# Stages B to F of a transformer block's backward pass on one core: new homes for transposed tiles, smaller loads, another queue for late transposes and stores

## The chip, the core and the metric

The kernel runs on one core of one Trainium2 chip. The metric is device time in microseconds (us), median over several executions. The page of a profile gives the "span" from the first to the last instruction; the time is some 1.7 us more. Each execution also records the mean granted clock of the matmul engine (TensorE).

## The reference

Forward and backward of one block: layer norm, linear attention with 32 heads of 20, output projection, residual, layer norm, gated MLP, residual. Outputs are the result and the gradients of x, wqkv, wo, w1, w3 and w2.

```python
x = A_x                                                # [1, 2048, 640] bf16
h = x + _A_ref(_layernorm(x), A_wqkv, A_wo)            # pq, pk = phi(q), phi(k); o = (pq.kv) / (pq.z)
h2 = h + _B_ref(_layernorm(h), A_w1, A_w3, A_w2)       # (silu(h.w1) * (h.w3)).w2, F = 1728   [names shortened]
_out, _vjp = jax.vjp(_f, A_x, A_wqkv, A_wo, B_w1, B_w3, B_w2)
return (_out, *_vjp(grad_out))
```

## The kernel before

The kernel fixes the order of instructions itself. The core's engines are TensorE (the matmul engine), VectorE, ScalarE, GpSimd and SyncE. SyncE issues almost all DMAs (transfers between the chip's main memory and the core's own; some transpose on the way), in the order of the text. A DMA that waited held up those behind it in that queue: in stage D below, one load is issued at 618.6 us behind two others that waited until 611.4 us. A tile framework adds the waits. Names: hh is the MLP's product and hb its transpose; g2 the output gradient; ggb the gradients at w1 and w3; g_h the gradient of h and ghT its transpose; gnd the gradient of the attention's numerator and denominator, gndT its transpose; pqb and pkb are rows of pq and pk. After stage A (forward and first half of the MLP's backward, to 361 us) come:

**Stage B**, the gradient of w2, and in its shadow the loads for C:

```python
load_hh(0)                                   # hb: 512 columns of hh, transposed by DMA
# [cut]
load_hh(1); load_hh(2)
for fc in range(FT):                         # 14 chunks of 128 rows, the last has FL = 64
    acc = ps.tile([P, 2, 512], F32, name="gw", bufs=4)
    for j in range(2):
        for t in range(ST):
            T.matmul(acc[:n, j, 0:HD], lhsT=hb[b][:, t, i*P:i*P+n], rhs=g2[:, t, j*HD:(j+1)*HD], ...)
    # [cut: copy to gw2o, store from ScalarE]
    if fc < CT: kvbd_T(*BLOCKS[fc])          # transposes of kv on the matmul engine
    if fc == 3: load_hh(3)
    if fc == 5: load_w13()                   # w13a, w13b: transposed by DMA
    if fc == 8: load_gg(0)                   # 1728 KB each
    if fc == 11: load_gg(1)
    if fc == FT - 2: w13_tail()
```

**Stage C**, one tile of 128 rows per step:

```python
for t in range(ST):
    b_load(t + 2); b_load_q(t - 1)                           # hnb, o_sb, pqb
    if t % 2 == 0 and 2 <= t <= ST - 4: load_gg(t // 2 + 1)  # for tiles t+2, t+3
    # three of six parts of ghn(t): 54 matmuls of 320 columns
    ln_rest.pop(t - 1)(); b_gT(t - 1)        # ghT: DMA transpose on SyncE
    b_gkv(t - 3)                             # part of ghn(t)
    b_go(t - 2)                              # reads ghT(t-2); part of ghn(t)
    b_gpq(t - 3)                             # reads gndT(t-3); part of ghn(t)
    b_gndT(t - 2)                            # gndT: DMA transpose on SyncE
```

**Stage D**, gradients of k and v; kT of chunk 3 takes the slot that chunk 0 leaves:

```python
    gphi(vaT[c][...], gkvT, pkb[c][:, i, :], g_k[:, t, :], d_acc)
    if t == TPC - 1: load_kT(3, ba, "ggb", 2)    # two DMA transposes
    if i == 3 and c + 2 < SC: load_pk(c + 2)     # pkb for tiles 8 to 11, then 12 to 15
```

**Stage E** is the gradient of x, with the last jobs of dwqkv between; **stage F** is 60 jobs of 16 matmuls for dw1 and dw3, on blocks of 288 columns loaded through DMA transposes.

## Time and profile before

| | |
|---|---|
| time, median of 3 (later 4) | 866.60 (866.23) us |
| span of the profile | 866.20 us |
| stage A, B, C | 361.0, 62.03, 148.06 us |
| stage D's loop, E (to the first job of F), F's matmul starts | 32.43, 108.69, 117.48 us |

The stages are measured in the trace from the first matmul of one to the first of the next (C to the last start of a ghn matmul; 32.93 us of projections follow before D's loop). Lines of the profile read: source line, engine, operation, output<-inputs, shapes, count, then busy us, mean ns of one, and idle time before. The lines that carry the argument stand in the prediction.

### The profile page before, as it was taken

The page shows a single profiled execution, that of the slowest core. Times are in us where ns is not written, and L with a number is a line of the kernel's source. Part 1 is how long each engine was busy: PE and PEld are TensorE (multiplying, and loading weights), DVE is VectorE, ACT ScalarE, POOL GpSimd, SP SyncE. Part 2 cuts the span into 40 slices and gives each one's busy share as a digit, 9 for nine tenths or more (in the row PEclk, how much of TensorE's full clock was granted, in tenths as well). Part 3 has the DMA queues.
Part 4 walks back from the last instruction along what each step waited for, and adds up shares of the span by engine and source line. Part 5 has one row for each costly group of instructions (what it writes and reads, how often), then busy time and mean ns, then how long its engine had stood idle before and what let it go on. Part 6 is the DMA issues. An engine that isn't in the chain of part 4 may idle for free.

```text
span 866.2 us, 15468 instructions
## 1 busy us (share of the span) xinstructions
PE 843.9 (97%) x6189; PEld 578.3 (67%) x6215; DVE 418.4 (48%) x946; ACT 326.7 (38%) x627; POOL 24.9 (3%) x42
## 2 busy tenths in 40 slices
PE   7999999999999999999999999999899999999998
PEld 4777544555555455777776777777677777777776
DVE  7786599877777565300145656654313343300000
ACT  4556866655555565011121121122422333322221
POOL 3100000000000000000000000000000000000000
PEclk9999999999999999999999999999999999999999
DMA  9978589364375652999787888799846588577661
GB/s 289 247 239 272 153 205 242 114 177 144 99 179 144 200 150 94 228 241 244 198 182 163 201 197 198 169 202 278 168 111 179 117 175 174 110 177 169 148 147 39
DMA packets 342279, 155.08 MB, mean 179 GB/s; under 512 B 242368, under 2 KB 340928, under 8 KB 342208
## 3 DMA queue, kind: packets, MB, share of 16 engines
q1 hardware_dynamic: 323696, 140.90, 68.5%
q10 hardware_dynamic: 18512, 13.20, 5.0%
q8 instruction: 48, 0.79, 0.4%
q14 instruction: 23, 0.19, 0.1%
HBM read 45.20 MB, written 50.02 MB: 110 GB/s over the span
## 4 chain that ended last, share of the span: by engine, by line
PE 76%; DMA 10%; ACT 1%; DVE 1%; issue 0%; SPq 0%; DVEq 0%; ACTq 0%
PE mm L414 19%; PE job L920 18%; PE ghn L684 10%; PE gxn L1009 8%; PE gw L630 7%; PE o L499 5%; DMA ghT<-g_h 5%; PE gwo L791 3%; DMA out_dram<-obs 2%; PE h L741 2%; PE at L371 2%; DMA hb<-hh_d 1%; DMA gg_d<-up 1%; DMA pkb<-pk_d 1%; PE dkv L968 1%; ACT obs L924 1%
## 5 line engine op out<-in xcount | busy, mean ns | idle before, releaser
L920 PE MATMUL job<-gb,hnN 128*128 128x288 bf16 x960 | 117.8, 286 | 0.0
L920 PEld LDWEIGHTS <-hnN 128*128 128x128 bf16 x960 | 93.9, 98 | 23.7
L684 PEld LDWEIGHTS <-ggb 128*128 128x128 bf16 x864 | 83.0, 98 | 31.1 <-DMA out_dram<-gw2o 0.3
L414 PE MATMUL mm<-pqT,w 128*128 128x512 bf16 x396 | 95.7, 379 | 0.5
L414 PEld LDWEIGHTS <-w 128*128 128x128 bf16 x540 | 52.4, 98 | 63.0 <-issue 2.3
L924 ACT CAST obs<-job 128x288 bf16<-128x288 f32 (+1 forms) x90 | 36.7, 407 | 128.8 <-PE job L920 68.0
L414 PE MATMUL mm<-g2T,w2T 128*128 128x512 bf16 x267 | 68.7, 379 | 0.6
L499 PE MATMUL o<-w,hhT 128*128 128x320 bf16 x448 | 67.5, 299 | 0.0
L1009 PE MATMUL gxn<-wqT,gT 128*128 128x320 bf16 x480 | 67.5, 299 | 0.0
L684 PE MATMUL ghn<-w13a,ggb 128*128 128x320 bf16 x448 | 65.6, 299 | 0.0
L684 PE MATMUL ghn<-w13b,ggb 128*128 128x320 bf16 x416 | 63.5, 299 | 0.0
L630 PE MATMUL gw<-g,hb 128*128 128x320 bf16 (+1 forms) x448 | 61.9, 299 | 0.4 <-DMA hb<-hh_d 0.4
L224 PE MATMUL big<-wqkv,pqT 128*128 128x320 bf16 x400 | 59.6, 308 | 0.8 <-ACT pqT L220 0.8
L224 PEld LDWEIGHTS <-pqT 128*128 128x128 bf16 x480 | 47.0, 100 | 19.1 <-ACT pqT L220 1.0
L499 PEld LDWEIGHTS <-hhT 128*128 128x128 bf16 x448 | 43.8, 98 | 23.6
L1009 PEld LDWEIGHTS <-gT 128*128 128x128 bf16 x480 | 47.0, 98 | 18.2
L920 PEld LDWEIGHTS <-g 128*128 128x128 bf16 x480 | 46.6, 98 | 17.5
L428 ACT CAST ghh<-mm 128x512 bf16<-128x512 f32 x56 | 32.8, 586 | 64.7 <-PE mm L414 39.2
L630 PEld LDWEIGHTS <-hb 128*128 128x128 bf16 (+1 forms) x448 | 43.8, 99 | 16.9 <-DMA hb<-hh_d 0.7
L707 ACT ACTIVATE y<-wb,s,ln_rs 128x640 bf16<-128x640 f32 x32 | 29.4, 920 | 65.8 <-DVE wb L703 65.8
L695 ACT ACTIVATE gs<-ghn 128x640 bf16<-128x640 f32 x16 | 11.2, 703 | 90.5 <-PE ghn L684 90.5
L414 PEld LDWEIGHTS <-w2T 128*128 128x128 bf16 x280 | 27.4, 98 | 25.6
(128 smaller groups left out, 1065.7 us busy)
## 6 DMA issues: line engine op xcount, KB each, us to landing
ggb<-gg_d SPq DMA_DIRECT2D x8, 1728.0 KB, 9.3
hh_d<-hhT SPq DMA_DIRECT2D x24, 256.0 KB, 2.4
gg_d<-gate SPq DMA_DIRECT2D x24, 256.0 KB, 2.5
gg_d<-up SPq DMA_DIRECT2D x24, 256.0 KB, 2.3
out_dram<-obs ACTq DMA_DIRECT2D x60, 72.0 KB, 2.8
va_d<-va SPq DMA_DIRECT2D x4, 768.0 KB, 6.1
out_dram<-gw2o ACTq DMA_DIRECT2D x18, 160.0 KB, 5.6
pk_d<-pkc SPq DMA_DIRECT2D x4, 640.0 KB, 4.5
```

Source lines behind the costliest of these rows:

```text
L224: T.matmul(acc, lhsT=pqT[:, c, t * P:(t + 1) * P], rhs=wqkv[:, c, n0:n0 + HD], start=(c == 0), stop=(c == DT - 1))
L371: T.matmul(at[:, 0:HD], lhsT=oT[t][:, c, :], rhs=wo[:, c, j * HD:(j + 1) * HD], start=(c == 0 and not on_pe), stop=(c == DT - 1))
L414: T.matmul(acc[:], lhsT=w[:, c, fc * P:(fc + 1) * P], rhs=rhs[:, c, :], start=(c == 0), stop=(c == DT - 1))
L428: A.copy(out=ghh[fc // 2][:, fc % 2, :], in_=acc[:])
L499: T.matmul(o2["ps"][:, 0:HD], lhsT=hhT[c][:, fc, i * P:(i + 1) * P], rhs=w2[:, fc, j * HD:(j + 1) * HD], start=(fc == 0), stop=(fc == FT - 1))
L630: T.matmul(acc[:n, j, 0:HD], lhsT=hb[b][:, t, i * P:i * P + n], rhs=g2[:, t, j * HD:(j + 1) * HD], start=(t == 0), stop=(t == ST - 1))
L684: T.matmul(acc[:, j, 0:HD], lhsT=ggb[t // 2][:, k, lo:lo + P], rhs=rhs[:, j * HD:(j + 1) * HD], start=(k == 0), stop=(k == NG - 1))
L707: A.activation(out=y[:], in_=wb[:], func=AF.Identity, bias=s[:, 3:4], scale=st.rs[:, t:t + 1])
L791: T.matmul(acc[m][:, j, 0:HD], lhsT=o_sb[:, t, m * P:(m + 1) * P], rhs=g_h[:, t, j * HD:(j + 1) * HD], start=(t == 0), stop=(t == ST - 1))
L920: T.matmul(acc[:, 0:n], lhsT=lhs[:, t, m * P:(m + 1) * P], rhs=rhs(t), start=(t == 0), stop=(t == ST - 1))
L924: A.copy(out=ob, in_=acc[:, 0:n])
L1009: T.matmul(acc[:, j, 0:HD], lhsT=gT[t][:, k, :], rhs=wqT[:, k, j * HD:(j + 1) * HD], start=(k == 0), stop=(k == 14))
```

## The change

Each part aims at a wait or at matmul work: the last, narrow chunk of dw2 with operands exchanged, so that 64 and not 320 columns stream; kv transposed by DMA early in dw2; the gradient loads (ggb) in halves, one in every tile; ghT and gndT on ScalarE's queue; x by single tiles; homes for kT of chunks 2 and 3 in space that is free already; stores of D and E on SyncE; blocks of 432 instead of 288 columns in F.

```diff
-NB, NBLK = 288, 6
+NB, NBLK = 432, 4
 # stage B
-    def kvbd_T(cc, dcs):            # [cut: T.transpose per block, V.tensor_copy]
+    def kvbd_T(m):
+        dmaT(out=kvbdT[:, :, m * P:(m + 1) * P], in_=kvbd[:, m, :])
+    def gw2_tail():
+        for c in range(DT):
+            for t in range(ST):
+                T.matmul(gt[:, c, :], lhsT=g2[:, t, c * P:(c + 1) * P], rhs=hb[3][:, t, P:P + FL], ...)
+        # [cut: copy; later 5 transposes and the store]
-    for fc in range(FT):
+    for fc in range(FT - 1):
-        if fc < CT:
-            kvbd_T(*BLOCKS[fc])
+        if fc == 2:
+            for m in range(DT):
+                kvbd_T(m)
 # stage C
-        if t % 2 == 0 and 2 <= t <= ST - 4:
-            load_gg(t // 2 + 1)
+        if 2 <= t <= ST - 3:
+            load_gg(t // 2 + 1, *((FT, NG) if t % 2 else (0, FT)))
-            dmaT(out=ghT[t][:], in_=g_h[:, t, :])
+            A.dma_start_transpose(out=ghT[t][:], in_=g_h[:, t, :])
-            dmaT(out=gndT[t][:], in_=gnd[t][:])
+            (A.dma_start_transpose if t < ST - 3 else dmaT)(out=gndT[t][:], in_=gnd[t][:])
 # stage D
-    load_kT(2, bv, "hnN", 1)
+    # [cut: kT(2) into the free part of wqT, kT(3) here; wqT loaded in thirds]
-        if t == TPC - 1:
-            load_kT(3, ba, "ggb", 2)
+        if t == 3 * TPC - 1:
+            load_wqT(1)
+            load_wqT(2)
 # stages D, E
-        A.dma_start(out=out, in_=ob)
+        q(out=out, in_=ob)                       # SyncE in D and E, ScalarE in F
-        A.dma_start(out=out1S[:, t, :], in_=gx[:])
+        dma(out=out1S[:, t, :], in_=gx[:])
 # [cut: x by tiles, hnN and block loads at other steps, order of jobs in E; w13_tail one chunk
#  earlier; blocks of F in 2 buffers of 432 columns instead of 3 of 288]
```

More of the change, by code (lines that the diff above doesn't have):

```diff
@@ L1 @@
+import itertools
 from contextlib import ExitStack
@@ L610, with load_gg, gw2_tail_out @@
     kvbdT = br.tile([P, CT, D], BF16, name="kvbdT")
-    def kvbd_T(cc, dcs):
-        tr = ps.tile([P, len(dcs), P], BF16, name="trk", tag="gw", bufs=4)
-        for i, dc in enumerate(dcs):
-            T.transpose(tr[:, i, :], kvbd[:, dc, cc * P:(cc + 1) * P], ident[:])
-        V.tensor_copy(out=kvbdT[:, cc, dcs[0] * P:(dcs[-1] + 1) * P].rearrange("p (i q) -> p i q", q=P), in_=tr[:])
-    ggb = {}
-    def load_gg(j):
-        ggb[j] = ba.tile([P, NG, 2 * P], BF16, name="ggb", bufs=2)
-        dma(out=ggb[j][:], in_=gg_d[:, j * 2 * P:(j + 1) * 2 * P].rearrange("(c p) w -> p c w", p=P))
-    for fc in range(FT):
+    def kvbd_T(m):
+        dmaT(out=kvbdT[:, :, m * P:(m + 1) * P], in_=kvbd[:, m, :])
+    ggb = {}
+    def load_gg(j, c0, c1):
+        if c0 == 0:
+            ggb[j] = ba.tile([P, NG, 2 * P], BF16, name="ggb", bufs=2)
+        dma(out=ggb[j][:, c0:c1, :],
+            in_=gg_d[c0 * P:c1 * P, j * 2 * P:(j + 1) * 2 * P].rearrange("(c p) w -> p c w", p=P))
+    gt = ps.tile([P, DT, FL], F32, name="gt", tag="gw", bufs=4)
+    def gw2_tail():
+        for c in range(DT):
+            for t in range(ST):
+                T.matmul(gt[:, c, :], lhsT=g2[:, t, c * P:(c + 1) * P], rhs=hb[3][:, t, P:P + FL],
+                         start=(c == 0 and t == 0), stop=(t == ST - 1), skip_group_check=True)
+        sb = br.tile([P, DT, FL], BF16, name="gts")
+        A.copy(out=sb[:], in_=gt[:])
+        return sb
+    def gw2_tail_out(sb):
+        tr = ps.tile([P, DT, P], BF16, name="gttr", tag="gw", bufs=4)
+        for c in range(DT):
+            T.transpose(tr[:FL, c, :], sb[:, c, :], ident[:])
+        ob = br.tile([P, D], BF16, name="gw2o", bufs=2)
+        A.copy(out=ob[:FL].rearrange("p (c n) -> p c n", c=DT), in_=tr[:FL])
+        A.dma_start(out=out_6[F - FL:F, :], in_=ob[:FL])
+    for fc in range(FT - 1):
         b, i = divmod(fc, 4)
-        n = P if fc < FT - 1 else FL
+        if fc == FT - 2:
+            sb = gw2_tail()
         acc = ps.tile([P, 2, 512], F32, name="gw", bufs=4)
@@ L629 @@
             for t in range(ST):
-                T.matmul(acc[:n, j, 0:HD], lhsT=hb[b][:, t, i * P:i * P + n], rhs=g2[:, t, j * HD:(j + 1) * HD],
+                T.matmul(acc[:, j, 0:HD], lhsT=hb[b][:, t, i * P:(i + 1) * P], rhs=g2[:, t, j * HD:(j + 1) * HD],
                          start=(t == 0), stop=(t == ST - 1))
+            if fc == FT - 2 and j == 0:
+                gw2_tail_out(sb)
         ob = br.tile([P, D], BF16, name="gw2o", bufs=2)
-        A.copy(out=ob[:n].rearrange("p (j n) -> p j n", j=2), in_=acc[:n, :, 0:HD])
-        A.dma_start(out=out_6[fc * P:fc * P + n, :], in_=ob[:n])
-        if fc < CT:
-            kvbd_T(*BLOCKS[fc])
+        A.copy(out=ob[:].rearrange("p (j n) -> p j n", j=2), in_=acc[:, :, 0:HD])
+        A.dma_start(out=out_6[fc * P:(fc + 1) * P, :], in_=ob[:])
         if fc == 3:
@@ L641 @@
         if fc == 8:
-            load_gg(0)
+            load_gg(0, 0, NG)
         if fc == 11:
-            load_gg(1)
-        if fc == FT - 2:
+            load_gg(1, 0, NG)
+        if fc == 2:
+            for m in range(DT):
+                kvbd_T(m)
+        if fc == FT - 3:
             w13_tail()
@@ L800, with load_x @@
     xnN = g2
-    def load_x(i):
-        sl = slice(i * TPC, (i + 1) * TPC)
-        dma(out=xnN[:, sl, :], in_=xS[:, sl, :])
+    def load_x(a, b):
+        dma(out=xnN[:, a:b, :], in_=xS[:, a:b, :])
     def norm_x(j):
@@ L809, with load_kT, ggb_kT @@
     pkT, vaT, pkb, gb = {}, {}, {}, {}
-    def load_kT(c, pl, tag, bufs):
-        kT = pl.tile([P, DT + CT, W], BF16, name="kT", tag=tag, bufs=bufs)
+    def load_kT(c, alloc):
+        kT = alloc()
         pkT[c], vaT[c] = kT[:, 0:DT, :], kT[:, DT:DT + CT, :]
         dmaT(out=pkT[c], in_=pk_d[c * W:(c + 1) * W, :])
+        yield
         dmaT(out=vaT[c], in_=va_d[c * W:(c + 1) * W, :])
+        yield
+    def ggb_kT():
+        return ba.tile([P, DT + CT, W], BF16, name="kT", tag="ggb", bufs=2)
+    kTg = itertools.chain(load_kT(0, ggb_kT), load_kT(1, ggb_kT))
     b_load(0)
@@ L851 @@
             b_gndT(u)
-        if t % TPC == 1 and t > TPC:
-            load_x(t // TPC - 1)
-        if t >= 2 * TPC - 1:
-            norm_x(t - 2 * TPC + 1)
+        if t >= 4:
+            load_x(t - 4, t - 3)
+        if t >= 6:
+            norm_x(t - 6)
         if t == ST - 2:
-            load_kT(0, ba, "ggb", 2)
+            next(kTg)
     b_load_q(ST - 1)
-    load_kT(1, ba, "ggb", 2)
+    for _ in kTg:
+        pass
     def part(n=1):
@@ L870, with load_wqT @@
     ln_rest.pop(a)()
-    load_x(SC - 1)
+    load_x(ST - 4, ST)
     wqT = U1.tile([P, 15, D], BF16, name="wqT", tag="D")
-    dmaT(out=wqT[:], in_=A_wqkv[:, :])
+    def load_wqT(k):
+        dmaT(out=wqT[:, k * DT:(k + 1) * DT, :], in_=A_wqkv[:, k * D:(k + 1) * D])
+    for _ in load_kT(2, lambda: wqT[:, DT:, :].rearrange("p k d -> p (k d)")[:, 0:(DT + CT) * W].rearrange(
+            "p (k w) -> p k w", w=W)):
+        pass
+    load_wqT(0)
     b_gT(b)
@@ L888 @@
     b_gpq(b)
-    for j in range(2 * TPC + 1, 3 * TPC):
+    for j in range(ST - 6, ST - 3):
         norm_x(j)
@@ L900 @@
     b_gpq(a)
-    for j in range(3 * TPC, ST):
+    for j in range(ST - 3, ST):
         norm_x(j)
@@ L910, in load_pk, with grad_job @@
         dma(out=pkb[c][:], in_=pk_v[:, c * TPC:(c + 1) * TPC, :])
-    obs = U1.tile([P, 10, 320], BF16, name="obs", tag="W6")
+    OB = DT * D
+    obs = U1.tile([P, OB], BF16, name="obs", tag="W6")
     cnt = [0]
     njob = 2
-    def grad_job(lhs, m, rhs, n, out):
+    def grad_job(lhs, m, rhs, n, out, q=dma):
         acc = ps.tile([P, 512], F32, name="job", bufs=njob)
@@ L921, in grad_job @@
                      stop=(t == ST - 1))
-        ob = obs[:, cnt[0] % 10, 0:n]
+        ob = obs[:, cnt[0] % (OB // n) * n:(cnt[0] % (OB // n) + 1) * n]
         cnt[0] += 1
         A.copy(out=ob, in_=acc[:, 0:n])
-        A.dma_start(out=out, in_=ob)
+        q(out=out, in_=ob)
     def half(src, j):
@@ L943 @@
     g_v = bv.tile([P, ST, D], BF16, name="g_v")
-    load_kT(2, bv, "hnN", 1)
+    for _ in load_kT(3, lambda: bv.tile([P, DT + CT, W], BF16, name="kT", tag="hnN")):
+        pass
     hnN = bv.tile([P, ST, D], BF16, name="hnN")
@@ L990, in load_block, with load_hnN @@
             base, _, f0 = blocks[i]
-            gb[i] = ex.tile([P, ST, NB], BF16, name="gb", bufs=3)
+            gb[i] = ex.tile([P, ST, NB], BF16, name="gb", bufs=2)
             dmaT(out=gb[i][:], in_=gg_d[base + f0:base + f0 + NB, :])
-    def load_hnN():
-        for i in range(SC):
-            dma(out=hnN[:, i * TPC:(i + 1) * TPC, :], in_=hn_v[:, i * TPC:(i + 1) * TPC, :])
+    def load_hnN(i):
+        dma(out=hnN[:, i * TPC:(i + 1) * TPC, :], in_=hn_v[:, i * TPC:(i + 1) * TPC, :])
     gT = {}
@@ L1012, in e_gxn @@
         ln_bwd(acc, t, xnN[:, t, :], ln1, gx[:], g_h[:, t, :], ex)()
-        A.dma_start(out=out1S[:, t, :], in_=gx[:])
+        return gx
     ps.release()
@@ L1022 @@
         e_T(0, k)
-    for t in (1, 2):
-        for k in range(3):
-            e_T(t, k)
-    load_hnN()
+    for k in range(3):
+        e_T(1, k)
+    next(jobs)
+    next(jobs)
+    for k in range(3):
+        e_T(2, k)
     for t in range(ST):
-        next(jobs, None)
-        e_gxn(t)
+        if t > 1:
+            next(jobs, None)
+        gx = e_gxn(t)
         if t + 3 < ST:
@@ L1032 @@
                 e_T(t + 3, k)
-        if t in (5, 9, 13):
-            load_block((t - 5) // 4)
+        dma(out=out1S[:, t, :], in_=gx[:])
+        if t in (2, 3, 5, 6):
+            load_hnN((2, 3, 5, 6).index(t))
+        if t in (8, 12):
+            load_block((t - 8) // 4)
     for _ in jobs:
@@ L1042 @@
     for i, (_, out, f0) in enumerate(blocks):
-        load_block(i + 3)
         for m in range(DT):
-            grad_job(hnN, m, lambda t: gb[i][:, t, :], NB, out[:, m, f0:f0 + NB])
+            grad_job(hnN, m, lambda t: gb[i][:, t, :], NB, out[:, m, f0:f0 + NB], A.dma_start)
+        load_block(i + 2)
     ps.release()
```

## The prediction

> **What bounds the kernel now.** I read the page first: busy shares, then the row of 40 slices.
>
> ```profile
> span 866.2 us, 15468 instructions
> PE 843.9 (97%) x6189; PEld 578.3 (67%) x6215; DVE 418.4 (48%) x946; ACT 326.7 (38%) x627; POOL 24.9 (3%) x42
> PE   7999999999999999999999999999899999999998
> PEclk9999999999999999999999999999999999999999
> L920 PE MATMUL job<-gb,hnN 128*128 128x288 bf16 x960 | 117.8, 286 | 0.0
> L630 PE MATMUL gw<-g,hb 128*128 128x320 bf16 (+1 forms) x448 | 61.9, 299 | 0.4 <-DMA hb<-hh_d 0.4
> ```
>
> The matmul engine is busy for 97% of the span at full clock; 22.3 us are not busy. So a change can only (a) take matmul work away, or (b) close one of few holes. The 299 ns of L630 is latency; start to start in the trace, 320 columns take 135.8 ns and 288 columns 122.5 ns. The second view, the waits of the matmul engine, names the holes:
>
> ```profile
> PE tr L218 <- DVE xn L144: 5.7, 1, 5.7
> PE dkv L968 <- DVE g_k L776: 3.1, 1, 3.1
> PE h L741 <- DMA ghT<-g_h: 2.3, 4, 0.9
> PE trh L408 <- DVE hn L144: 1.9, 4, 0.8
> PE mm L414 <- ACT up L447: 1.8, 1, 1.8
> ```
>
> The first is the program's start; it, the fourth and the fifth lie before 300 us, in code that the change leaves alone. That leaves the second and third. Measured as start-to-start time above the normal spacing, they are 3.25 us (at 622 us) and 1.07+0.73+0.53+0.63 = 2.96 us (at 470, 490, 509 and 529 us). The third view, the timeline of the SyncE queue, tells what stands behind them:
>
> ```profile
> 359.17 24.11 SPq L581 DMA_TRANSPOSE hb<-hh_d  x3
> 384.52 9.83 SPq L601 DMA_TRANSPOSE w13a<-in_B_w_dram  x1
> 394.46 11.69 SPq L602 DMA_TRANSPOSE w13b<-in_B_w_dram  x1
> 406.24 5.50 SPq L622 DMA_DIRECT2D ggb<-gg_d  x2
> ...
> 460.14 0.39 SPq L622 DMA_DIRECT2D ggb<-gg_d  x1
> 460.65 6.13 SPq L720 DMA_TRANSPOSE ghT<-g_h  x1
> ...
> 470.78 1.21 SPq L720 DMA_TRANSPOSE ghT<-g_h  x1
> ...
> 611.39 2.95 SPq L815 DMA_TRANSPOSE kT<-pk_d  x1
> 614.39 4.04 SPq L816 DMA_TRANSPOSE kT<-va_d  x1
> 618.56 1.23 SPq L910 DMA_DIRECT2D pkb<-pk_d  x2
> ```
>
> The ghT transpose queued straight behind a 1728 KB ggb load takes 6.13 us to issue (1.21 us when no load is ahead) and lands 10.7 us after its start, against 2.6 us. And the pkb load for tile 8 stands behind two kT transposes that wait for the slot of chunk 0: issued at 618.56, landed at 624.7, while the matmuls stop at 622.1. Two single-queue hold-ups, each in front of a saturated engine.
>
> [...]
>
> **The change part by part.** Stages: B = dw2 (361 to 423 us), C = gradient through w1/w3 (to 597), D = gradients of k and v (to 640), E = gradient of x (to 745), F = the jobs for dw1/dw3 (to the end). Instructions before B are the same.
>
> 1. *B, last chunk of dw2.* Removed: 32 matmuls of 320 columns, 4.35 us by the chain of 32 in the trace. Added: 80 matmuls of 64 columns, [...]2.33 us; and 5 transposes of 128 columns, 0.28 us. Net -1.74 us. Open point: each of the 80 needs its own weight load. In the trace one load behind a 20-column matmul holds nothing up (next start after 28 ns), but the longest run of such small pairs is about a dozen.
> 2. *B, kvbd.* 12 transposes on the matmul engine go: 12 x 55.8 ns = -0.67 us. In their place 5 DMA transposes of 128x768, the size of gndT, which takes 1.2 us to issue: 5 x 1.25 = 6.2 us on SyncE, between the third hb and the last one. There the queue idles only 0.4 us, so all behind it moves by about 5.8 us. The DMA share in 360 to 420 us is 1.17 to 1.22 in the windows view, so it will not be caught up. ggb(0) landed at 415.5 and would land at about 421.3; stage C would begin at 423.1-1.74-0.67 = 420.7. So a new hole of about 0.6 us, with hnb and the rest behind it: +1.0 us with a margin.
> 3. *C, ghT and gndT on ScalarE, gg in halves, x by tiles.* [...]-2.96 us. ScalarE pays 25 or so issues of 1.2 us in a stage in which it is busy 3.4 of 20 us; in the built order the next PSUM read stands ahead of gndT's wait, so nothing on the matmul path waits for it: 0.
> 4. *D, homes of kT.* No slot is waited for at t=3; kT(3) is loaded at the start and pkb(2) is issued as soon as tile 3 is done: -3.25 us. The wqT thirds 2 and 3 wait for tile 11, are issued near 619 (a third of 12.51 us each) and land about 20 us before their first use: 0.
> 5. *E, stores on SyncE.* Its queue had 3.7 us of transposes per 6.25 us tile; two stores add 0.7 us, still below 6.25. The 432-column block load at t=8 takes some 7.9 us to issue (between 4.9 for 288 and 9.6 for 512) and pushes the transposes of tile 12 to about 1.5 us before their use: +0.3 us as a chance.
> 6. *F, blocks of 432.* 960 x 122.5 = 117.6 us[...]: -0.8 us. A block is issued when its slot is free, one block (5 x 16 x 182.5 ns = 14.6 us) before its use; 288 columns landed in 7.8 us, 512 in 12.3 to 14.2, so 432 in about 11: hidden. The last copy and store are half as large again: +0.25 us.
>
> Sum: -1.74-0.67+1.0-2.96-3.25+0.3-0.8+0.25 = -7.9 us. From 866.6: 858.7; I predict 859.0, as the small costs can only add.
>
> **The rivals.** *A: the B stage turns DMA-bound.* SyncE is full there and now gets 6 us more, while the matmuls end 2.4 us earlier. For it: share above 1.1 and ggb's 7.6 us margin almost used up. Against it: only ggb(0) is needed at once; ggb(1) has 18 us more. If w13b and ggb were slowed too, the hole would be 3 us: 861.5. *B: small pairs are held to the weight loads or to the issue.* If 80 pairs took 55 ns each, as the 128-column transposes do, the tail saves nothing: 860.5. *C: ghT still comes late*, because [...]the ggb halves now come in every iteration. For it: C's DMA share is 0.8 to 0.9. Against it: the needed time fell short by only about 1 us of 10.7, and half a load ahead is 4 us less. If half the hole stays: 860.4. *D: all waits go and the ggb hole does not come*: 857.5. *E: SyncE head of line in E*, a store waiting for the layer norm in front of a transpose: the store is ready about 4.3 us after its tile's matmuls, before the next slot comes free at 6.25, so I give it little; if each tile lost 0.3 us: 863.
>
> **Range and chances.** The removable total is 9.4 us, a bound of 857.2 before costs; the likeliest rivals cost 1 to 3 us each. Low 857.0, high 862.5 for 8 in 10. Faster by over 2% needs 849.3, more than all that is removable: 0.01. Slower by over 2% needs 884, a new bound that no view hints at: 0.01. Within 2%: 0.98.
>
> **What would show it.** Right: no wait of h on ghT; none of dkv on g_k near 620 us; 80 matmuls in about 2.3 us at the end of dw2; gb matmuls 182 ns apart without a gap at a block's start; ghn's first matmul waiting 0 to 2 us for ggb. Wrong: ghT landing over 8 us on ScalarE's queue, a tail of 4 us, gaps at the blocks of F, or gaps in E while SyncE sits in a store. The total would be wrong if the hole at the start of C exceeded 4 us, since nothing later gives that back.

The sum came to -7.9 us, 858.7 from 866.6. The 2.33 us of step 1 and the -0.8 us of step 6 (117.6 us becomes 116.8) rest on the spacing of matmuls of 64 and 432 columns, which the kernel before does not have. An estimate from its trace gives the same: matmuls start 135.8 ns apart at 320 columns and 55.8 at 128, and the straight line through these two gives 29.1 ns at 64 (80 of them 2.33 us) and 182.5 at 432 (640 of them 116.8 us). It also gives 122.5 at 288, as measured, but the 28 ns measured at 20 columns lie well above it, so 64 was the less certain. The -2.96 us of step 3 is the sum of the four measured waits; that all of them would go on ScalarE's queue was the estimate.

## The result, and the profile after

The changed kernel took 863.42 us (862.22 to 864.59, 4 runs) against 866.23. A ratio here is the mean time of one kernel's fast runs over that of the other's in the same rounds, so not quite the ratio of the medians: 0.9967 (95% interval 0.9949 to 0.9984). Within 2%, as forecast, but outside the range of 857.0 to 862.5. More than half of the expected gain is missing.

The page of the changed kernel, for the same rows as before:

```profile
span 862.8 us, 14882 instructions
PE 842.6 (98%) x5936; PEld 545.9 (63%) x5936; DVE 416.1 (48%) x940; ACT 322.8 (37%) x608; POOL 25.0 (3%) x42
L960 PE MATMUL job<-gb,hnN 128*128 128x432 bf16 x640 | 117.0, 346 | 0.0
L651 PE MATMUL gw<-g,hb 128*128 128x320 bf16 x416 | 57.0, 299 | 0.0
```

The busy share even rose. But busy time does not tell how fast the work went, as will be seen. The waits of the matmul engine (us in total, times, longest):

```profile
PE ghn L708 <- DMA ggb<-gg_d: 3.2, 1, 3.2
PE mm L415 <- ACT up L448: 2.3, 1, 2.3
...
PE h L765 <- DMA ghT<-g_h: 1.0, 2, 0.7
```

The wait of dkv is gone and that of ghT is smaller, but apart from the program's start a new one of 3.2 us tops the list: stage C's first matmul waits for its first ggb load. The timeline of the matmul engine around it (start, duration):

```profile
412.76 2.50 PE L630 MATMUL gt<-hb,g 128*128 128x64 bf16 x80
415.09 2.34 PE L651 MATMUL gw<-g,hb 128*128 128x320 bf16 x16
417.64 0.47 PE L639 MATMUL gttr<-ident,gts 128*64 128x128 bf16 x5 [0.21 <-ACT gts L633]
418.04 2.35 PE L651 MATMUL gw<-g,hb 128*128 128x320 bf16 x16
423.56 1.71 PE L708 MATMUL ghn<-w13a,ggb 128*128 128x320 bf16 x10 [3.18 <-DMA ggb<-gg_d]
```

The 80 small matmuls start 29.2 ns apart, as hoped. All that they saved is then spent waiting. SyncE's timeline says why ggb is late:

```profile
378.21 7.74 SPq L614 DMA_TRANSPOSE kvbdT<-kvbd  x5
386.05 4.10 SPq L582 DMA_TRANSPOSE hb<-hh_d  x1
...
391.40 11.08 SPq L602 DMA_TRANSPOSE w13a<-in_B_w_dram  x1
402.58 10.28 SPq L603 DMA_TRANSPOSE w13b<-in_B_w_dram  x1
412.91 6.25 SPq L621 DMA_DIRECT2D ggb<-gg_d  x2
```

Five transposes of kv, 7.74 us, stand in front of the last hb load, and everything behind is pushed back: the first ggb load is issued at 412.9 where it was 406.2, and lands at 423.5 where it was 415.5. Last, the windows around the hole (stretch, busy us of the matmul engine, its weight loads, VectorE, ScalarE and GpSimd with counts, then granted clock, DMA share, GB/s):

```profile
420.00:424.00 4.00, 0.82 (x7) 0.38 (x6) 0.00 (x0) 0.69 (x1) 0.00 (x0) 1.00 1.16 327
424.00:428.00 4.00, 4.00 (x21) 2.40 (x18) 0.00 (x0) 0.69 (x1) 0.00 (x0) 0.60 1.20 293
428.00:432.00 4.00, 4.00 (x30) 2.89 (x29) 0.00 (x0) 0.00 (x0) 0.00 (x0) 0.98 0.62 204
```

After the hole the engine is "busy" for the full 4 us, yet does 21 matmuls instead of 30: the granted clock falls to half at 424.8 us, stays there for 3.41 us, and 13 matmuls start 267 ns apart instead of 136. That is 13 x 131 ns = 1.7 us, seen in no wait.

By stages, in us (A's code is the same; it differs from run to run):

| stage | before | after | after, second profile |
|---|---|---|---|
| A | 361.0 | 360.3 | 359.0 |
| B | 62.03 | 63.24 | 62.56 |
| C | 148.06 | 148.74 | 147.07 |
| D loop | 32.43 | 28.67 | 28.67 |
| E | 108.69 | 108.69 | 108.69 |
| F | 117.48 | 116.62 | 116.62 |
| last matmul to end | 3.59 | 3.64 | 3.62 |

D and F gave what was expected. B and C together were to save 4.4 us (the prediction's steps 1 to 3); they took 1.9 us more than before in the first profile and 0.5 us less in the second. (The two first profiles are of executions of 867.99 and 864.59 us, 1.8 and 1.2 us above their medians; so the stages are compared, and not these totals.)

### The profile page after: what moved, and what is told of

Same layout as the page of the kernel before. It is cut to its first block, busy times and chain, and to the rows that moved or that the text cites. A ratio compares the mean times of both kernels' runs of the same rounds, so it can differ in the third digit from the quotient of the medians.

```text
span 862.8 us, 14882 instructions
## 1 busy us (share of the span) xinstructions
PE 842.6 (98%) x5936; PEld 545.9 (63%) x5936; DVE 416.1 (48%) x940; ACT 322.8 (37%) x608; POOL 25.0 (3%) x42
## 4 chain that ended last, share of the span: by engine, by line
PE 77%; DMA 5%; SPq 3%; DVE 2%; ACT 1%; issue 0%; ACTq 0%; DVEq 0%
PE job L960 21%; PE mm L415 19%; PE ghn L708 10%; PE gxn L1050 8%; PE o L500 7%; PE gw L651 3%; PE gwo L815 3%; DMA ghT<-g_h 2%; PE h L765 2%; PE at L372 2%; SPq L602 1%; DMA ggb<-gg_d 1%; SPq L603 1%; DMA gg_d<-up 1%; DMA kT<-pk_d 1%; PE dkv L1009 1%
## 5 line engine op out<-in xcount | busy, mean ns | idle before, releaser
L960 PE MATMUL job<-gb,hnN 128*128 128x432 bf16 x640 | 117.0, 346 | 0.0
L960 PEld LDWEIGHTS <-hnN 128*128 128x128 bf16 x640 | 62.6, 98 | 54.1
L964 ACT CAST obs<-job 128x432 bf16<-128x432 f32 (+1 forms) x70 | 33.3, 476 | 123.8 <-PE job L960 123.8
L651 PE MATMUL gw<-g,hb 128*128 128x320 bf16 x416 | 57.0, 299 | 0.0
L651 PEld LDWEIGHTS <-hb 128*128 128x128 bf16 x416 | 40.6, 98 | 15.7
L719 ACT ACTIVATE gs<-ghn 128x640 bf16<-128x640 f32 x16 | 11.3, 704 | 90.6 <-PE ghn L708 81.8
```

The source lines that it names most:

```text
L651: T.matmul(acc[:, j, 0:HD], lhsT=hb[b][:, t, i * P:(i + 1) * P], rhs=g2[:, t, j * HD:(j + 1) * HD], start=(t == 0), stop=(t == ST - 1))
L960: T.matmul(acc[:, 0:n], lhsT=lhs[:, t, m * P:(m + 1) * P], rhs=rhs(t), start=(t == 0), stop=(t == ST - 1))
L964: A.copy(out=ob, in_=acc[:, 0:n])
```

## The experiments

Three theories. **1:** the place of the kv transposes in SyncE's queue makes the hole, and the hole makes the half clock. **2:** what cured the ghT waits is the other queue (my prediction) or the halves. **3:** the hole near 298 us that all kernels share is another case of theory 1. All runs gave correct results. "Stage" figures are from each run's profile.

| run | time, median (range) us | ratio to before (95%) | A | B | C | D |
|---|---|---|---|---|---|---|
| after_again | 863.17 (860.47 to 867.84) | 0.9968 (0.9942 to 0.9994) | 359.0 | 62.56 | 147.07 | 28.67 |
| kvbd_pe | 859.45 (857.34 to 860.76) | 0.9915 (0.9897 to 0.9933) | 359.5 | 60.29 | 145.44 | 28.67 |
| old_tail | 859.92 (859.41 to 862.25) | 0.9933 (0.9916 to 0.9950) | 363.6 | 61.36 | 145.05 | 28.66 |
| gg0_halves | 861.58 (859.39 to 864.49) | 0.9951 (0.9929 to 0.9973) | 360.8 | 61.08 | 146.72 | 28.67 |
| pk_first | 865.99 (862.36 to 867.76) | 0.9996 (0.9971 to 1.0021) | 362.9 | 62.02 | 148.07 | 29.01 |
| kvbd_late | 859.58 (857.08 to 861.88) | 0.9922 (0.9900 to 0.9943) | 358.6 | 59.62 | 147.32 | 28.67 |
| pe_spT | 858.24 (856.72 to 860.63) | 0.9915 (0.9894 to 0.9936) | 360.1 | 60.30 | 145.04 | 28.67 |
| pe_whole_gg | 865.95 (865.09 to 870.28) | 1.0008 (0.9986 to 1.0031) | 361.4 | 60.30 | 153.89 | 28.67 |
| pk_first_again | 863.76 (863.06 to 866.82) | 0.9966 (0.9941 to 0.9991) | 362.8 | 62.02 | 148.78 | 29.01 |
| pe_spT_again | 857.59 (856.64 to 860.44) | 0.9895 (0.9870 to 0.9920) | 363.0 | 60.30 | 145.04 | 28.67 |
| g2_spread | 855.71 (855.22 to 856.25) | 0.9867 (0.9843 to 0.9892) | 357.8 | 60.29 | 145.04 | 28.67 |
| stores_act | 860.53 (858.42 to 867.90) | 0.9935 (0.9896 to 0.9974) | 361.1 | 60.30 | 147.48 | 29.01 |

The rows were run on three chips, each with its own runs of the kernel before (medians 866.58, 865.58 and 866.86). One profile's total differs by 2 us or more from another's for A alone, so stage figures tell more than spans.

### after_again: the changed kernel once more

No edit.

> The changed kernel once more, unaltered, as the mark for the other three runs of this call. Theory 1 (the hole before the first ghn matmul is 3.3 us long[...]): times spread by about 2 us, 862.2 to 864.6, and a profile in which the hole is present every time, with a mean clock of either 0.997 (half clock after the hole) or about 1.0 (none). Rival (the spread is ordinary chip noise): no relation between time and mean granted clock.

The hole was there again (2.94 us above the normal spacing), and again half clock for 3.41 us after it. Of the 10 executions of the changed kernel, the two with a mean clock of 1.0 took 862.22 and 860.47 us; the eight with 0.996 to 0.998 took 860.91 to 867.84, mean 864.0. So half clock occurred in most runs, but not in all; the mean clock does not tell whether behind this hole or behind the one near 298 us (theory 3). The times spread over 7.4 us, where I expected about 2.

### kvbd_pe: kv back on the matmul engine

```diff
-        if fc == 2:
-            for m in range(DT):
-                kvbd_T(m)                  # DMA
+        if fc < CT:
+            kvbd_T(*BLOCKS[fc])            # T.transpose, as before the change
```

> The changed kernel with the 12 kv transposes back on the matmul engine and no DMA transposes of kv. Theory 1 (the five DMA transposes held SyncE from 378.2 to 386.0 us and pushed the first ggb load back by about 8 us): ggb(0) lands near 415.5 us, the 3.3 us hole goes to 0, the clock stays full (1.7 us), and the 12 transposes cost 0.67 us: about 4.4 us faster than the changed kernel, near 859. Rival (the queue would be late anyway, because the three loads in stage B and the wide w13 transposes are limited by the DMA engines, not by the queue): the hole stays at 2 us or more, and the time is within 1 us of the changed kernel.

Median 3.7 us below the changed kernel on the same chip. The hole is gone from the waits, and the clock stays full to the end of the matmuls. SyncE's timeline, against the one above:

```profile
382.67 9.48 SPq L602 DMA_TRANSPOSE w13a<-in_B_w_dram  x1
392.25 10.10 SPq L603 DMA_TRANSPOSE w13b<-in_B_w_dram  x1
402.45 5.51 SPq L624 DMA_DIRECT2D ggb<-gg_d  x2
```

The first ggb load now lands 52.6 us after the start of B (63.2 with the kv transposes in front). Stage B is 60.29 us, 2.95 less than in the changed kernel (2.27 less than in its second profile) although it has 0.67 us more matmul work. The first half of theory 1 holds, at its size: the place in the queue makes the hole. Stage C also fell, to 145.44: its ghT waits vanished too.

### old_tail: more matmul work

```diff
-    for fc in range(FT - 1):               # and the tail as 80 matmuls of 64 columns
+    for fc in range(FT):                   # the tail as 32 matmuls of 320 columns, as before the change
```

> The changed kernel with the last chunk of dw2 in its old form (32 matmuls of 320 columns, 1.7 us more work). Theory 1 (stage C starts when ggb(0) lands, whatever the matmuls did before[...]): the hole shrinks to about 1.6 to 1.9 us, ghn starts at the same time as before, the clock stays full in every run, so the kernel with MORE work is 1.5 us FASTER than the changed kernel in its throttled executions and equal to it in the others. Rival (the saving of 1.74 us is real and the hole is fixed): 1.7 us slower.

The kernel with 1.7 us more work was 3.2 us faster by median (the intervals of the two ratios overlap). The direction is that of theory 1; its size is more than I expected: the hole did not shrink to 1.6 us but went altogether, because ggb(0) landed 61.1 us after the start of B here (62.5 and 63.2 in the two profiles of the changed kernel). Why it lands 1.5 to 2 us earlier I can't show; 1.2 us of it lie between issue and landing (9.4 us against 10.6), and the times of ScalarE's stores are one difference. The half clock in this run's profile (mean 0.998) lies in stage A, at 302 us, behind a hole of 2.76 us. Stage B is 61.36 us without a wait for ggb. That the clock would stay full behind a shorter hole was a guess, and this run could not test it, as there was no hole there. So the saving of the tail is real work saved, and worth nothing while stage C starts when a load lands.

### gg0_halves: the first ggb load in two

```diff
-            load_gg(0, 0, NG)
+            load_gg(0, 0, FT)
+            load_gg(0, FT, NG)
```

> The changed kernel with the first ggb load split in two like the later ones, so that ghn can begin on the first half. Theory 1: the first half (896 of 1728 KB) lands about 3 us earlier, the hole falls below 1 us, the clock stays full; 3 to 4.5 us faster than the changed kernel, near 860. Rival (both halves are served together, so that the first half lands hardly earlier, or ghn waits for the second half instead): hole moves inside ghn's first tile, under 1 us gained.

Partly. The first half landed at 418.3 us, before it was needed, and the hole before ghn and the half clock after it were gone from the profile. But another wait of 1.5 us came up in front of the tail's transposes, for ScalarE's copy (which stood behind a store that ScalarE issued at 418.4 us, just after that first half had landed), and later one of 1.3 us for a second half of ggb. Median 1.6 us better, less than the 3 to 4.5 expected and not clear of the noise (the intervals of the ratios overlap widely): the queue was as late as ever, only the first load was smaller.

### kvbd_late: the same DMA transposes behind the two ggb loads

```diff
-        if fc == 2:                        # [moved behind load_gg(1, 0, NG) at fc == 11]
-            for m in range(DT):
-                kvbd_T(m)
```

> The changed kernel with the five DMA transposes of kv left on SyncE but issued behind the two first ggb loads instead of in front of the last hb load. Theory 1 (what hurt was their place in the queue, in front of ggb(0), not the method): ggb(0) lands about 55 us after the start of stage B as with the matmul engine's transposes, no hole before ghn, full clock; total like that kernel or 0.7 us better, 858.5 to 859.5. Rival (the DMA transposes as such are costly, because they load the DMA engines or delay hnb and pqb behind them): a wait appears in the first tiles of stage C, and the total is 861 or more.

Stage B fell to 59.62 us, the shortest of all: no hole, and 0.67 us less than with the matmul engine's transposes, which is exactly their 12 x 55.8 ns. So the method cost no matmul time; the place did. The total is that of kvbd_pe within the noise; this profile's stage C shows two ghT waits (1.64 and 0.62 us, at 521 and 542 us), kvbd_pe's none. They are far from the kv transposes, and the next runs show where such waits come from.

### pe_whole_gg: ScalarE's queue without the halves

Base: kvbd_pe.

```diff
-        if 2 <= t <= ST - 3:
-            load_gg(t // 2 + 1, *((FT, NG) if t % 2 else (0, FT)))
+        if t % 2 == 0 and 2 <= t <= ST - 4:
+            load_gg(t // 2 + 1, 0, NG)
```

> The same kernel (kv on the matmul engine) with ghT and gndT on ScalarE's queue, but the ggb loads whole again, in every second tile. Theory 2 (the other queue cures it): stage C stays within 0.3 us of 145.4. Rival ([...]a whole load slows the transpose in the other queue as well, and the halves were needed): ghT waits of 1 to 3 us in the tiles with a load.

The rival won, and by more than it claimed: stage C takes 153.89 us, 8.4 us more than with halves and 5.8 us more than the kernel before, which had everything in one queue (and x in larger loads, which was not tried apart). The waits of the matmul engine:

```profile
PE h L798 <- DMA gndT<-gnd: 5.1, 4, 1.7
PE h L767 <- DMA ghT<-g_h: 2.4, 1, 2.4
```

and the landing of ghT, from the view of that tile:

```profile
DMA to landing us min/median/max: 2.6/9.1/11.9
```

Before the change ghT landed after 4.2 us in the median and 10.7 at most. In the other queue the issue is short (1.2 us), but the landing is not earlier. And the load suffers as well: the ggb load issued at 440.8 us, with ghT issued 0.2 us later from ScalarE, landed after 15.7 us; the corresponding load of the kernel before, with ghT behind it in the same queue, landed after 8.8 us. Over all six whole loads of stage C it is 11.3 to 15.7 us, against 8.6 to 10.3. What slows them is not shown.

### pe_spT: the halves without ScalarE's queue

Base: kvbd_pe.

```diff
-            A.dma_start_transpose(out=ghT[t][:], in_=g_h[:, t, :])
+            dmaT(out=ghT[t][:], in_=g_h[:, t, :])
-            (A.dma_start_transpose if t < ST - 3 else dmaT)(out=gndT[t][:], in_=gnd[t][:])
+            dmaT(out=gndT[t][:], in_=gnd[t][:])
```

> The kernel with kv transposed on the matmul engine (the best so far, stage C 145.4 us without a single ghT wait), but with ghT and gndT issued from SyncE again; the ggb loads stay in halves. Theory 2 (the transpose must not stand behind a ggb load in the same queue): with half a load in front in every tile the ghT waits come back in part, 1 to 3 us in stage C. Rival (the halves alone cure it, the other queue is worth nothing): stage C stays within 0.3 us of 145.4.

The rival won again: stage C is 145.04 us without one ghT wait, here, in pe_spT_again and in g2_spread. With ScalarE's queue, the same code for C gave 145.05 to 148.74 us in the profiles (145.44 in kvbd_pe, 147.48 in stores_act; the two profiles of the changed kernel hold 1.7 us of half clock each). By time the two kernels can't be told apart (858.24 and 859.45 us, on two chips). Landing of ghT with halves in one queue:

```profile
DMA to landing us min/median/max: 2.8/6.8/8.2
```

and 2.6/8.0/10.0 with the transposes on ScalarE's queue (kvbd_pe). So the halves did it (the loads of x by single tiles, which both have, were not tried apart); the second queue is worth nothing here and makes C less even.

### pk_first and pk_first_again: the kernel before, two loads exchanged

```diff
-        if t == TPC - 1:
-            load_kT(3, ba, "ggb", 2)
         if i == 3 and c + 2 < SC:
             load_pk(c + 2)
+        if t == TPC - 1:
+            load_kT(3, ba, "ggb", 2)
```

> The kernel BEFORE the change with one edit: in stage D the load of pkb(2) is issued ahead of the two kT transposes of chunk 3 instead of behind them. Theory (queue order alone made the hole at tile 8): the 3.25 us wait of dkv on g_k is gone, stage D falls from 32.4 us to about 28.7 us (what the changed kernel has), and the time falls by 3.2 to 3.8 us, so the new homes of kT were not needed for it. Rival (pkb was late for another reason, or kT of chunk 3 is now late in its place): the wait stays or moves to the matmuls that read kT at tile 12, and less than 2 us are gained.

In the profile the loop of stage D fell from 32.43 to 29.01 us and the dkv wait was gone. The timed runs showed nothing: ratio 0.9996. In that profile stage A was 1.9 us longer than in the one of before, with half clock after a hole of 2.85 us near 298 us.

> The same one-edit kernel as in the run with pkb(2) loaded first, once more, because its profile had stage D 3.4 us shorter but its timed runs were no faster than before. If the saving is real and the first timing was chance (a hole near 298 us that all kernels share, with or without half clock after it): 1.5 to 3.4 us faster this time, stage D again near 29.0 us. If the shorter D of the profile is the exception and the timed runs are the rule: a ratio within 0.2% of 1 again.

Ratio 0.9966, and D 29.01 again. The pooled picture is a gain of about 1.5 us in the timed runs and 3.4 us in the stage; the 3.2 to 3.8 us expected were not seen in the timed runs, and the interval of neither excludes 2 us. That the queue order alone removes the wait is shown by both profiles: no new homes were needed for that.

### stores_act: the stores of D and E back on ScalarE

Base: kvbd_pe.

```diff
-    def grad_job(lhs, m, rhs, n, out, q=dma):
+    def grad_job(lhs, m, rhs, n, out, q=A.dma_start):
-        dma(out=out1S[:, t, :], in_=gx[:])
+        A.dma_start(out=out1S[:, t, :], in_=gx[:])
```

> The kernel with kv on the matmul engine (859.5, ratio 0.9915) with the stores of stages D and E back on ScalarE. Theory (the stores were never on the path; ScalarE is busy a third of stage E): stage E and the total within noise of that kernel. Rival (the stores on SyncE freed ScalarE for the layer norm, or on the contrary hold up SyncE's transposes): E changes by over 0.5 us.

Stage E did not move: 108.69 us to the first job of F, as in all others but one (109.01 in pe_spT). D's loop went from 28.67 to 29.01 us, which both profiles of pk_first also show, with their stores on ScalarE; so the stores on SyncE are worth 0.34 us there. The total is inconclusive (one run of 867.9 us, wide interval, and C was 2.0 us longer than in kvbd_pe, with waits of 1.6 us for a half of ggb and 0.7 us for ghT).

### pe_spT_again and g2_spread: the common hole near 298 us

All kernels so far wait 0.8 to 2.9 us near 298 us, for ScalarE's copy into `up`. ScalarE waits for the store of the buffer's last content (3.7 us in the kernel before), and in SyncE's queue that store stands behind four 640 KB loads of the output gradient, which is not needed before stage B: issued at 292.21 us, it landed after 7.72 us, where the median of these stores is 2.3.

> The fastest kernel so far (kv on the matmul engine, transposes on SyncE, ggb in halves) as the mark for the next run: 858 to 859, stage C near 145.0 us, and a hole of 0.8 to 2.8 us near 298 us that differs from run to run.

857.59 us, with a hole of 2.8 us at 298 us in its profile. The windows behind it show half clock as after the hole of the changed kernel (columns as above):

```profile
296.00:300.00 4.00, 2.26 (x11) 0.92 (x10) 0.45 (x1) 0.00 (x0) 0.00 (x0) 1.00 0.89 309
300.00:304.00 4.00, 3.12 (x12) 1.59 (x12) 0.69 (x1) 3.03 (x6) 0.00 (x0) 0.71 0.05 15
304.00:308.00 4.00, 3.95 (x18) 1.77 (x17) 3.86 (x7) 1.45 (x3) 0.00 (x0) 0.86 0.46 150
```

The edit of g2_spread, on top of that kernel:

```diff
             if c == SC - 1 and fc == 0:
                 g2 = U1.tile([P, ST, D], BF16, name="g2", tag="Q")
-                for i in range(SC):
-                    dma(out=g2[:, i * TPC:(i + 1) * TPC, :], in_=goS[:, i * TPC:(i + 1) * TPC, :])
+            if c == SC - 1 and fc % 2 == 1 and fc < 2 * SC:
+                i = fc // 2
+                dma(out=g2[:, i * TPC:(i + 1) * TPC, :], in_=goS[:, i * TPC:(i + 1) * TPC, :])
```

> That kernel with the four 640 KB loads of the output gradient in stage A issued one in every second step instead of all four in a row. Theory 3 (the common hole near 298 us is again a small store that stands behind bulk loads in SyncE's queue: the store of up lands at 299 and frees the buffer that ScalarE waits for): the hole goes, stage A shrinks by 1 to 2.8 us, half clock after it no longer occurs, and the times spread less; about 856.5. Rival (the wait has another cause, or one load at a time is enough to hold the store): the hole stays or splits into several, less than 0.7 us gained.

855.71 us, ratio 0.9867, against 0.9895 of its base in the same rounds. The waits of the matmul engine:

```profile
PE tr L219 <- DVE xn L145: 6.6, 2, 5.7
PE trh L409 <- DVE hn L145: 1.9, 4, 0.8
PE tr L360 <- DVE o_t L348: 0.9, 1, 0.9
```

Neither `up`, nor ggb, nor ghT, nor dkv is left. Stage A shrank to 357.8 us, the profile shows no half clock before the last matmuls are done, and five runs lie within 1.0 us of each other where the other kernels of these calls spread over 2.8 to 9.5. Theory 3 holds. This version beats both kernels: 11.2 us under the kernel before, and 7.5 under the changed one by the medians on two chips.

## Why the prediction was right or wrong

| step | predicted us | measured us, profile after against before |
|---|---|---|
| 1 tail of dw2 | -1.74 | the 80 took 2.33 as forecast; a wait of 0.38 for ScalarE's copy was added |
| 2 kv transposes | -0.67 and +1.0 | -0.67 (kvbd_late against kvbd_pe) and +3.34 (2.94 in the second profile), **and +1.7 of half clock** |
| 3 ghT, gndT, ggb | -2.96 | -1.2: waits of 1.33 on ghT and 0.45 on gnd remained; -2.62 once the queue in front was not late (kvbd_pe); -3.02 with the transposes back on SyncE (pe_spT) |
| 4 homes of kT | -3.25 | -3.76, of which 3.41 by order alone and 0.34 by the stores |
| 5 stores in E | +0.3 | 0 |
| 6 blocks of 432, end | -0.8 and +0.25 | -0.86 and +0.05 |

The step that failed is 2, "a new hole of about 0.6 us ... +1.0 us with a margin". Its mechanism was right, down to the load that would be waited for, and its term of the sum was mis-sized threefold, for two reasons. I took five transposes at 1.25 us, as gndT is issued in stage C, and the landing of ggb as it was. In stage B's loaded queue the five took 7.74 us (single issues 1.2 to 2.3), so that ggb(0) was issued 7.35 us later after the start of B than before and not 5.8; and it took 10.6 instead of 9.2 us to land. (The two w13 transposes behind them were not slower in sum: 21.4 us against 21.5. Why the landing took longer is open: in old_tail, with the same queue in front, it took 9.4.) A duration measured in another stage was too short here. Rival A named 861.5 for this, but I gave it too little room. And the clock was missing from the sum: I read it off the page as full and took it for given, while in the changed kernel it was half for 3.41 us behind the new hole of 3.34 us. So the total missed although the hole stayed under the 4 us that the prediction named as its limit. 2.3 us more of hole and 1.7 us of clock are 4.0 of the 4.4 us between 863.42 and 859.0. The remaining waits of step 3 (1.8 us) and the tail's 0.4 us are mostly offset by D (0.5), by small costs that did not come (0.5) and by a shorter A (0.7).

Step 3 came out near its number in the end, but by luck: its reason was wrong. I held the place behind a load in the same queue to be the cause, so that a second queue would cure it, and left rival C (ghT still late there) at half the hole. The runs show the reverse: the second queue without the halves makes C 5.8 us longer than before, the halves in one queue make it 3.0 us shorter. The prediction's own sign against it, ghT landing over 8 us on ScalarE's queue, was there: 10.4 us at most in the changed kernel. The last ghT cost something as well: ScalarE stood 8.37 us in front of it and issued it at 564.60 us, just after SyncE's first kT had landed (564.54), some 7 us behind the rhythm of the others, and the wait of 0.45 us on gnd follows it (570.65). Steps 1, 4, 5 and 6 stand. The chances stand too: nothing came near 2% in either direction.

How a hole leads to half clock is only partly settled. Where the hole was gone (in front of ghn in kvbd_pe and gg0_halves, near 298 us in g2_spread), so was the half clock after it, but the length of a hole alone does not decide. Of the holes in the profiles (idle time above the normal spacing), 2.76 (old_tail), 2.78 (pe_spT_again), 2.85 (pk_first), 2.85 (pk_first_again), 2.94 (after_again) and 3.34 us (the changed kernel) were followed by half clock; 3.24 was not, nor was one of 2.48 at 298 us in the changed kernel. The one of 3.24 us is in the kernel before, at 622 us, and its windows (columns as above) show full clock after it:

```profile
620.00:624.00 4.00, 2.28 (x22) 1.69 (x20) 0.00 (x0) 1.01 (x3) 0.00 (x0) 1.00 0.97 295
624.00:628.00 4.00, 2.63 (x29) 2.11 (x29) 2.48 (x6) 1.51 (x4) 0.00 (x0) 1.00 1.26 183
628.00:632.00 4.00, 4.00 (x47) 3.24 (x45) 1.68 (x4) 1.84 (x5) 0.00 (x0) 1.00 0.18 44
```

What decides it is not shown. Two things can be read off the two traces side by side. In the 3.41 us before the half clock of the changed kernel (421.37 to 424.79 us) the matmul engine was busy for 1.22 us; around the hole of the kernel before, it was busy for 1.58 us from 620.70 to 624.11 and for 2.15 us from there to 627.52. And by the clock records, the changed kernel had full clock for 413.01 us, half for 3.413, then full for 433.49; the kernel before had full clock for 853.33 us, to the end of its matmuls. The three full stretches are 121, 127 and 250 times 3.413 us to within 0.1 us. This was read off afterwards, no run tested it, and it makes no rule.

## What to carry to other kernels

Work taken off a saturated engine is worth nothing if the next stage starts when a load lands (the 1.7 us of the tail here); look first at what the queue must deliver, and count every DMA put in front of that load with its duration in the loaded queue (five transposes took 7.74 us, not 6.2). Big loads in pieces, spread out, and urgent small DMAs ahead of them did more here than a second queue (stage C 145.04 us against 153.89). And a hole of about 3 us in the matmul engine can cost more than its length, as six of seven holes of 2.76 us and more did here: compare the granted clock, and the count of matmuls in a window, after each hole.
